# Seven products in four of six feature pairs of the middle tiles, with banks that change parts

## The chip, the cores and the metric

The kernel runs on one core of a Trainium2 chip. A core has five engines that run side by side, each with its own queue of instructions in a fixed order: TensorE (PE; its weight loads are listed as PEld), VectorE (DVE), ScalarE (ACT), GpSimd (POOL) and SyncE (SP, which here only issues DMAs). They meet through semaphores. Matrix products land in PSUM, which has eight banks of 512 fp32 columns on 128 partitions; everything else is in SBUF. The metric is device time in microseconds (us), lower is better. The kernel before took 323.42 us, the median of three runs (322.38, 323.42 and 326.44).

## The reference

Eight batches of eight heads go through sparse attention, and the result through a bilinear feed-forward layer:

```python
scores = scale * np.matmul(q, k.transpose(0, 1, 3, 2))          # (8, 8, 576, 576), head_dim 64
mask_local = (rel >= 0) & (rel < stride)                          # stride 32, heads 0 to 3
mask_strided = (rel >= 0) & (pos[None, :] % stride == pos[:, None] % stride)   # heads 4 to 7
attn = softmax(np.where(masks, scores, -1e9))
x = np.matmul(attn, v).transpose(0, 2, 1, 3).reshape(4608, 512)
a = x @ w_a                                                       # (512, 1536)
b = x @ w_b
out = (a * b) @ w_out                                             # (1536, 512), float32
```

## The kernel before, in words

**Tiles and slots.** The 4608 tokens are nine tiles of 512 (t = 0 to 8). A tile has sixteen slots: twelve for the features f = 0 to 11, 128 features each, in which a and b are made and multiplied into `pf` (`ffn_ab`), and four for the output y (`ffn_ys` for tiles 1 to 8). The attention of batch t + 1 is spread over the slots of tile t. So each engine's queue is one list, written in the order in which the program emits the slots and steps; no planner moves anything.

**Steps of the attention.** `STEPS`, `LATER` and `IN_Y` (lines 578 to 587) give the place of each step. A position is a slot; -4 to -1 are slots of the tile before, and x.5 is the middle of a slot. The letters, with the unit u = 0 to 7 behind them (0 to 3 local heads, 4 to 7 strided ones):
- S: the score products into the banks `st`, three or four of them (line 378), then their exponential on ScalarE (line 398), then the mask, an AND on VectorE of p with the mask (line 416, both in SBUF). "s" is S without the mask, and "m" is the mask alone.
- V: the products with v into bank `o` (line 459); VectorE takes a reciprocal and normalises (lines 467 and 485). For u of 4 and over, `step_VT` writes banks `o` and `e` (line 518), ScalarE takes logarithms and an exponential (530, 531), VectorE multiplies into `xT` (533).
- Q: a copy of query rows from `qT` into `qz` on VectorE (line 334), two for the local heads and two for the strided ones (Q2, Q3).
- O and I: rows out to DRAM and back transposed, both by DMAs of SP.

**a and b.** A plain feature f is four products of 512 columns for a and four for b (line 621), a bank each; in tile 4, whose tokens wrap round in `xT`, each is two products of 256. ScalarE copies a to `a_sb` (line 642), VectorE multiplies it with b (line 645). `mm_bank` (line 607) deals out four banks in turn, three of a pool "mm" and one of a pool "tp"; `o`, `e` and the two of `st` are the other four.

**A seven-product pair.** Features 2g and 2g + 1 form pair g. In `a_pair_mid` (lines 680 to 738) a is made for both features of a pair by seven products of half the contraction and half the tokens (two matmuls of 256 columns each) in place of eight, of sums of weights (`wsum_a`) and differences of x (`xsum`). They go into three half banks: X takes four of the seven in turn, each time copied out by ScalarE into a quarter of `a_sb`; Y takes one, which VectorE adds to quarter (0, 0); Z takes two: the first is copied to `p7`, both are added to quarters of the second feature. b1 and b0 are the b banks of the second and first feature, eight matmuls of 512 columns (line 706). VectorE multiplies `mult(1)` with b1, then `mult(0)` with b0 (line 711). The pair is a generator: its first half, up to `yield p7`, is the slot f = 2g, the rest the slot f = 2g + 1. `MID_A` (line 28) gives pairs 1 and 3 of tiles 3 to 6 this form. Pairs of tiles 7 and 8 have it too, in `a_pair`, a similar function, with no attention beside them and with one addition on GpSimd (line 791).

**y.** It also takes seven products, of stage sums and differences of `pf` that VectorE makes in `fast_s` (line 824; both inputs in SBUF), n = 0 to 3, in slices of the six pairs: [0, 2), [2, 4), [4, 6), some of them as one. Lines 1072 to 1076 and 1122 to 1125 give their slots.

**GpSimd's queue.** GpSimd issues the loads of k, q and v, each behind a copy of one element named `pace` (line 1138), which waits for the slot's last result and so ties the load to the slot. In tiles 3 to 5, slot 2 issues two loads (`kr`, `qr`, line 208), slot 9 one of v (219), slots 11 to 14 four more (237), slot 14 two large ones (210). A pacing copy stands in the queue in each slot that has anything of the tables at the end of the program (`at`, lines 1067 to 1125), stage differences included.

Of the kernel before, what the change touches and what calls it, by code (L numbers as in the profile page):

```python
# [7 lines left out]
F32 = mybir.dt.float32  # L8
BF16 = mybir.dt.bfloat16
I16 = mybir.dt.int16  # L10
ALU = mybir.AluOpType
# [11 lines left out]
PAD = 32  # L23
PW = 344
VW = 128
WCH = (0, 2, 5, 9, 12)
FAST_Y = (1, 2, 3, 4, 5, 6, 7, 8)
MID_A = {t: (1, 3) for t in (3, 4, 5, 6)}
FAST_A = {7: (1, 2, 3, 4, 5), 8: (0, 1, 2, 3, 4, 5)}


# [1 line left out]
def kernel(  # L33
# [10 lines left out]
    nc = tc.nc  # L44
# [6 lines left out]
    KD = d_model // 128  # L51
    FD = d_ff // 128
    TTOK = 512
    NT = n_tok // TTOK
    HL = H // 2
    W = S // 2

    const = ctx.enter_context(tc.tile_pool(name="const", bufs=1))
# [3 lines left out]
    fsb = ctx.enter_context(tc.tile_pool(name="ffn", bufs=2))  # L62
# [3 lines left out]
    psum4 = {}  # L66

    def open_psum(stack, **bufs):
        for nm, n in bufs.items():
# [12 lines left out]
    qT = (const.tile([128, 2, S], BF16, name="qTl"), const.tile([128, HL * W], BF16, name="qTs"))  # L82
    kT_buf = [(const.tile([128, 2, PAD + S], BF16, name=f"kT{i}l"), const.tile([128, 2, RS * GP + 48], BF16, name=f"kT{i}s"))
              for i in range(2)]
    vl_buf = [const.tile([128, HL * 6, VW], BF16, name=f"vl{i}") for i in range(2)]

    p_buf = [const.tile([128, 2, PW], BF16, name=f"p{i}") for i in range(5)]
    vs_buf = [const.tile([NP, HL, RS, VW], BF16, name=f"vs{i}") for i in range(2)]
# [77 lines left out]
    HT = TTOK // 2  # L166
# [5 lines left out]
    def fast_w(n, gs):  # L172
        a, b = ((wov[:, 0, 1], wov[:, 0, 0]), (wov[:, 1, 1], wf[:, 0]), (wov[:, 1, 1], wov[:, 0, 1]),
                (wov[:, 1, 0], wf[:, 1]))[n]
        nc.vector.tensor_tensor(wf[:, n, gs], a[:, gs], b[:, gs], op=ALU.subtract)
# [389 lines left out]
    def F_mm(f, w, kk):  # L565
# [18 lines left out]
    LATER = {-4: "Q0", -3: "Q1", -1: "S0", 0: "S1", 1: "V0", 2: "S2", 3: "V1 Q2 O0", 4: "S3 Q3", 5: "V2", 6: "S4", 7: "V3 O1 I0", 8: "S5", 9: "V4 I1",  # L584
             10: "S6",
             11: "V5"}
    IN_Y = {2: "S7", 6: "V6", 11: "V7"}
    FN = {"Tk": step_Tk, "Tq": step_Tq, "S": step_S, "V": step_V, "X": step_X, "W": lambda b, n: fast_w(n, slice(0, 3)),
          "s": S_px, "m": S_m, "L": lead_vl, "O": rows_out, "I": rows_in, "Pk": lambda b, c: pair_up("k", c), "Pq": lambda b, c: pair_up("q", c),
          "Q": lambda b, n: step_Q(b, n // 2, n % 2)}  # L590
# [6 lines left out]
    steps = {}  # L597

    def take(pos):
        for b, names in steps.get(pos, ()):  # L600
            run(b, names)
# [5 lines left out]
    def mm_bank(shape):  # L607
        nm = "tp" if used[0] % 4 == 3 and used[0] >= 0 else "mm"
        used[0] += 1
        return psum4[nm].tile(shape, F32, tag=nm, name="mm")  # L610
# [13 lines left out]
    def ffn_ab(t, f, mid, ab=None):  # L624
        if f == 0:
            pfs[t] = fsb.tile([128, FD, TTOK], BF16, tag="pf", name="pf", bufs=1)
        pf = pfs[t]
        if f // 2 in FAST_A.get(t, ()) + MID_A.get(t, ()):
            if f % 2 == 0:
                pairs[t, f // 2] = (a_pair_mid if t in MID_A else a_pair)(t, f // 2)  # L630
            return next(pairs[t, f // 2])
        if ab is None:
            ab = [mm_bank([128, TTOK]) for _ in range(2)]
            if f == 0:

                late = 1 if t == 1 else 3
                for kks in ((0, 2, 3), (1,)) if t == 1 else ((0, 2), (1,), (3,)):
                    ab_mm(t, f, ab, kks, last=kks[-1] if kks[-1] == late else -1)
            else:
                ab_mm(t, f, ab, range(KD), mid)  # L640
        a_sb = fsb.tile([128, TTOK], F32, tag="a_sb", name="a_sb", bufs=3)
        nc.scalar.copy(a_sb, ab[0])  # L642
        if t in FAST_Y:
            halves = lambda x: x.rearrange("p (a i s) -> p a i s", i=2, s=16)
            nc.vector.tensor_mul(pf[:, f, :].rearrange("p (i a s) -> p a i s", i=2, s=16), halves(a_sb), halves(ab[1]))  # L645
        else:
            nc.vector.tensor_mul(pf[:, f, :], a_sb, ab[1])
        return pf[:1, f, :1]
# [31 lines left out]
    def a_pair_mid(t, g):  # L680

        pf = pfs[t]
        X = psum4["e"].tile([128, 512], F32, tag="e", name="e")[:, :HT]
        Y, Z, b1, b0 = [mm_bank([128, TTOK]) for _ in range(4)]
        Y, Z = Y[:, :HT], Z[:, :HT]
        a = [fsb.tile([128, TTOK], F32, tag="a_sb", name="a_sb", bufs=3) for _ in range(2)][::-1]
        p7 = fsb.tile([128, HT], F32, tag="p7", name="p7")
        quarter = lambda e, k: a[e][:, HT * k:HT * (k + 1)]

        def P(bank, lhs, rhs, start=False):  # L690
            for c in range(2):
                nc.tensor.matmul(bank, lhsT=lhs(c), rhs=rhs(c), start=start and c == 0, stop=c == 1, skip_group_check=True)  # L692

        w = lambda e, j: (lambda c: wav[:, j, c, g, e])
        ws = lambda n: (lambda c: wsum_a[n][:, c, g])
        x = lambda j, k: (lambda c: x_part(t, j, k)[:, c])
        xs = lambda n: (lambda c: xsum[t][:, n, c])

        def b_mm(bank, e, kks):
            f = 2 * g + e  # L700
            x0 = TTOK * t % (XR * S)
            for kk in kks:
                for k in range(2) if x0 + TTOK > XR * S else (None,):
                    rhs = x_part(t, kk // 2, k)[:, kk % 2] if k is not None else xT[:, kk, x0:x0 + TTOK]
                    dst = bank if k is None else bank[:, HT * k:HT * (k + 1)]
                    nc.tensor.matmul(dst, lhsT=wb_sb[:, kk, 128 * f:128 * (f + 1)], rhs=rhs,  # L706
                                     start=kk == 0 and k in (None, 0), stop=kk == KD - 1 and k in (None, 1))

        def mult(e, bank):
            halves = lambda v_: v_.rearrange("p (a i s) -> p a i s", i=2, s=16)  # L710
            nc.vector.tensor_mul(pf[:, 2 * g + e, :].rearrange("p (i a s) -> p a i s", i=2, s=16), halves(a[e]), halves(bank))

        def add(q, other):
            nc.vector.tensor_tensor(q, other, q, op=ALU.add)

        P(Y, w(0, 1), x(1, 0), True)
        P(X, w(0, 0), x(0, 0), True)
        nc.scalar.copy(quarter(0, 0), X)
        b_mm(b1, 1, (0, 1, 2))
        P(X, ws(1), xs(1))  # L720
        nc.scalar.copy(quarter(1, 0), X)
        P(Z, ws(2), xs(2), True)
        nc.scalar.copy(p7, Z)
        b_mm(b1, 1, (3,))
        add(quarter(0, 0), Y)
        yield p7[:1, :1]
        P(X, ws(0), xs(0))
        nc.scalar.copy(quarter(1, 1), X)
        b_mm(b0, 0, (0,))
        P(Z, w(1, 1), xs(3))  # L730
        add(quarter(1, 0), Z)
        add(quarter(1, 1), p7)
        b_mm(b0, 0, (1, 2, 3))
        P(X, ws(3), x(1, 1))
        nc.scalar.copy(quarter(0, 1), X)
        mult(1, b1)
        mult(0, b0)
        yield pf[:1, 2 * g, :1]

    def a_pair(t, g):  # L740
# [2 lines left out]
        pool, nm = ((pst, "st"), (psum4["o"], "o"))[g % 2]  # L743
        X = pool.tile([128, 512] if nm == "o" else [128, 2, 512], F32, tag=nm, name="ax")
        X = X[:, :HT] if nm == "o" else X[:, 0, :HT]
        a = ([fsb.tile([128, TTOK], F32, tag="a_sb", name="a_sb", bufs=3) for _ in range(2)] if g % 2 == 0 else
             [t.rearrange("p h n -> p (h n)")[:, :2 * TTOK].bitcast(F32) for t in kT_buf[0]])
        got = {k: psum4[nm].tile([128, TTOK], F32, tag=nm, name="mm")
               for k, nm in zip((1, "Z", "Y", 0), (("mm", "mm", "tp", "mm"), ("tp", "mm", "mm", "mm"))[g % 2])}
# [64 lines left out]
    def fast_s(t, n, gs):  # L814
        if t not in pss:
            pss[t] = nat.tile([128, FG * 5 * SW], BF16, tag="shared", name="ps").rearrange("p (n g m) -> p n g m", g=FG, n=5)
        s = pss[t][:, :, gs, :HT]
        x = pfs[t].rearrange("p (g e) (i m) -> p e i g m", e=2, i=2)[:, :, :, gs]
        a, b, op = ((x[:, 0, 1], x[:, 1, 1], ALU.add), (s[:, 0], x[:, 0, 0], ALU.subtract),
                    (x[:, 0, 0], x[:, 0, 1], ALU.subtract), (x[:, 1, 0], s[:, 1], ALU.subtract))[n]  # L820
        if (t, n) == (NT - 1, 2) and {gs.start, gs.start + 1} <= set(FAST_A[t]):
            later[t, gs.start] = lambda: nc.gpsimd.tensor_tensor(s[:, n], a, b, op=op)
            return
        nc.vector.tensor_tensor(s[:, n], a, b, op=op)  # L824
# [156 lines left out]
    with tc.manual_schedule(engines={ENG.PE, ENG.SP, ENG.Pool, ENG.DVE, ENG.Activation}):  # L981
# [76 lines left out]
        for t in range(NT):  # L1058
            slots += [(ffn_ab, t, f) for f in range(FD)] + [(ffn_ys if t in FAST_Y else ffn_y, t, j) for j in range(4)]
        for b in range(1, B):  # L1060
            for pos, names in (STEPS.get(b) or {16 * (b - 1) + x: n for x, n in LATER.items()}).items():
                steps.setdefault(pos, []).append((b, names.split()))
            if b not in STEPS:
                for n, names in IN_Y.items():
                    steps["y", b - 1, n] = [(b, names.split())]

# [53 lines left out]
            for n in range(4):  # L1120
                do(16 * (NT - 1) + 2 * g + 1, fast_s, NT - 1, n, slice(g, g + 1))
        for t in FAST_Y[:-1]:
            for slot, n, z0, z1 in ((4, 0, 0, 2), (5, 2, 0, 2), (6, 1, 0, 2), (7, 3, 0, 2), (8, 2, 2, 4), (9, 0, 2, 4),
                                    (10, 1, 2, 4), (12, 3, 2, 6)):
                do(16 * t + slot, fast_s, t, n, slice(z0, z1))
        for i, (fn, t, j) in enumerate(slots):
# [45 lines left out]
```

## Time and profile before

| | |
|---|---|
| median of three runs | 323.42 us |
| the profiled execution | 322.75 us, span 321.0 us from first to last instruction |
| granted TensorE clock, mean | 0.997 |
| busy: PE, DVE, ACT, POOL | 312.5, 251.3, 193.0, 116.7 us |
| matmuls of line 621, 128 x 512 and 128 x 256 | 480 and 128 |
| matmuls of the eight seven-product pairs, lines 692 and 706 | 112 and 80 |
| VectorE, mean of one: multiplication (645), add of a quarter (714), mask (416), stage difference 512 wide (824) | 681, 414, 452, 418 ns |
| ScalarE, mean of one: copy of 512 (642), of 256 (718), exponential (398) | 585, 372, 650 ns |
| GpSimd, mean of one addition in tiles 7 and 8 (791) | 730 ns |

Rows of a profile name the line of the program, the engine, the operation, and the tile written with the tiles read, as in `mm<-xT,wa_sb`; behind the operation stand the shapes. A timeline row begins with the start and the length in us, and brackets at its end give the idle time of the engine before it and who ended that. In a chain row the first two figures are the start and the time that this piece of the chain holds. The duration of one matmul includes its way through the array, so durations overlap; the step from start to start is what one costs when they follow each other. VectorE and ScalarE also start the next instruction some 0.05 to 0.1 us before the last has ended, where nothing is waited for.

### The profile page before, as it was taken

Reading aid. Unit: us, or ns where it says so; the run is one execution under the profiler, and the core shown is the slowest. Engines: PE = TensorE matmul, PEld = TensorE weight load, DVE = VectorE, ACT = ScalarE, POOL = GpSimd, SP = SyncE. Lnnn points to the kernel's source line nnn. Section 1 sums busy time; section 2 is a strip of 40 time slices with the busy share of each in tenths; the row PEclk is TensorE's granted clock in tenths of the full one; section 3 lists DMA queues with packets and bytes.
Section 4 is the critical chain, followed back from the end, with each engine's and each line's share of the span. In section 5 each row is a group of like instructions: output and inputs, shape, how many; then the busy total and the mean of one; then the engine's idle time right before and its main releaser. Section 6 shows DMA issues by size and latency. Waiting matters only on the chain.

```text
span 321.0 us, 7265 instructions
## 1 busy us (share of the span) xinstructions
PE 312.5 (97%) x2742; PEld 215.5 (67%) x2742; DVE 251.3 (78%) x574; ACT 193.0 (60%) x374; POOL 116.7 (36%) x207
## 2 busy tenths in 40 slices
PE   8799999999999999999999999999999999999994
PEld 5664555455865577567999985569665966786683
DVE  6787886588778898898689868996899668857962
ACT  6873776455754576557655865577556755435541
POOL 8754711780264264315540435033101012203520
PEclk9999999999999999999999999999999999999998
DMA  8999999999399999999999999999153040004004
GB/s 149 176 205 193 204 184 198 203 112 192 61 145 173 261 117 63 126 90 214 142 130 157 191 126 101 102 231 153 12 151 57 2 131 2 0 3 132 0 2 132
DMA packets 127059, 40.31 MB, mean 126 GB/s; under 512 B 114864, under 2 KB 124144, under 8 KB 126832
## 3 DMA queue, kind: packets, MB, share of 16 engines
q0 software_dynamic: 79760, 19.20, 67.7%
q1 hardware_dynamic: 47120, 20.59, 36.4%
q8 instruction: 21, 0.34, 0.5%
q14 instruction: 14, 0.11, 0.1%
q10 hardware_dynamic: 144, 0.07, 0.1%
HBM read 38.93 MB, written 18.28 MB: 178 GB/s over the span
## 4 chain that ended last, share of the span: by engine, by line
PE 92%; DMA 2%; POOL 2%; DVE 1%; ACT 1%; issue 0%; POOLq 0%
PE mm L621 35%; PE mm L890 20%; PE mm L770 6%; PE mm L706 4%; PE st L378 4%; PE mm L952 3%; PE ax L763 3%; PE o L459 2%; DMA tk<-in_v_dram 2%; PE mm L763 2%; PE e L692 2%; PE mm L917 2%; PE mm L692 2%; PE o L518 1%; POOL shared L201 1%; PE end L917 1%
## 5 line engine op out<-in xcount | busy, mean ns | idle before, releaser
L621 PE MATMUL mm<-xT,wa_sb 128*128 128x512 bf16 (+1 forms) x304 | 72.1, 356 | 0.0
L621 PE MATMUL mm<-xT,wb_sb 128*128 128x512 bf16 (+1 forms) x304 | 72.0, 357 | 0.0
L642 ACT COPY a_sb<-mm 128x512 f32<-128x512 f32 x68 | 39.8, 585 | 29.5 <-PE mm L621 26.4
L1138 POOL CAST pace<-pf 1x1 f32<-1x1 bf16 x68 | 19.7, 290 | 88.7 <-DVE pf L645 44.2
L621 PEld LDWEIGHTS <-wb_sb 128*128 128x128 bf16 x304 | 29.3, 98 | 26.5 <-DMA wb_sb<-in_moe_w_b_dram 0.2
L645 DVE TENSOR_TENSOR pf<-a_sb,mm 128x512 bf16<-128x512 f32 x58 | 39.5, 681 | 9.4 <-ACT a_sb L642 5.8
L398 ACT ACTIVATE p<-st 72x576 bf16<-72x576 f32 (+1 forms) x56 | 36.4, 650 | 15.4 <-PE st L378 14.7
L621 PEld LDWEIGHTS <-wa_sb 128*128 128x128 bf16 x304 | 27.3, 98 | 17.4
L890 PEld LDWEIGHTS <-ps 128*128 128x128 bf16 x336 | 32.7, 98 | 3.7
L890 PE MATMUL mm<-wf,ps 128*128 128x256 bf16 x252 | 29.8, 273 | 0.0
L855 ACT COPY y_sb<-mm 128x512 f32<-128x512 f32 (+1 forms) x32 | 17.9, 559 | 19.1 <-PE mm L890 15.7
L1138 POOL COPY pace<-y_sb 1x1 f32<-1x1 f32 x22 | 9.6, 438 | 52.9 <-DVE y_sb L853 27.2
L770 PE MATMUL mm<-xT,wb_sb 128*128 128x512 bf16 x88 | 26.2, 379 | 0.0
L890 PEld LDWEIGHTS <-pf 128*128 128x128 bf16 x252 | 23.5, 98 | 2.7
L237 POOL DMA_DIRECT2D vs<-in_v_dram x24 | 21.7, 907 | 4.6 <-issue 3.1
L890 PE MATMUL mm<-wo_sb,pf 128*128 128x256 bf16 x168 | 21.8, 273 | 0.0
L824 DVE TENSOR_TENSOR ps<-pf 128x512 bf16<-128x512 bf16 (+1 forms) x49 | 19.6, 400 | 0.8
L706 PE MATMUL mm<-xT,wb_sb 128*128 128x512 bf16 (+1 forms) x80 | 19.1, 336 | 0.0
L416 DVE TENSOR_TENSOR p<-p,mask_l 128x576 int16<-128x576 int16 x32 | 14.5, 453 | 5.8 <-ACT p L398 5.5
L533 DVE TENSOR_TENSOR xT<-o,xr 64x288 bf16<-64x288 f32 x16 | 7.7, 480 | 13.5 <-ACT xr L531 13.4
L459 PEld LDWEIGHTS <-p 128*128 128x128 bf16 (+1 forms) x256 | 13.0, 97 | 7.5 <-DVE p L416 1.2
L416 DVE TENSOR_TENSOR p<-p,mask_s 72x576 int16<-72x576 int16 x28 | 12.6, 451 | 1.9 <-ACT p L398 1.7
(211 smaller groups left out, 639.2 us busy)
## 6 DMA issues: line engine op xcount, KB each, us to landing
out_dram<-y_sb SPq DMA_DIRECT2D x14, 512.0 KB, 5.4
kr<-in_k_dram POOLq DMA_DIRECT2D x12, 288.0 KB, 6.9
qr<-in_q_dram POOLq DMA_DIRECT2D x12, 288.0 KB, 8.1
vl<-in_v_dram POOLq DMA_DIRECT2D x6, 384.0 KB, 7.8
out_dram<-y_sb SPq DMA_DIRECT2D x7, 256.0 KB, 3.7
vs<-in_v_dram POOLq DMA_DIRECT2D x24, 72.0 KB, 5.6
xd<-xl SPq DMA_DIRECT2D x12, 144.0 KB, 5.7
wo_sb<-in_moe_w_out_dram POOLq DMA_DIRECT2D x4, 384.0 KB, 11.3
```

The source lines that it names most:

```text
L237: nc.gpsimd.dma_start(out=vs_buf[b % 2][:, h, :, 0:D], in_=v[b, HL + h].rearrange("(p r) d -> p r d", r=RS))
L398: nc.scalar.activation(p_flat(p)[:M, :2 * W].rearrange("p (i n) -> p i n", n=2 * n), st[:M].rearrange("p a (i n) -> p (a i) n", n=256)[:, ...
L416: nc.vector.tensor_tensor(pi, pi, mk, op=ALU.bitwise_and)
L459: nc.tensor.matmul(of[:, j, i, :w], lhsT=pt, rhs=vt, start=True, stop=True)
L621: nc.tensor.matmul(ps_[:, c0:c0 + n], lhsT=w[:, kk, 128 * f:128 * (f + 1)], rhs=xT[:, kk, x0:x0 + n], start=(kk == first and c0 == 0), sto ...
L642: nc.scalar.copy(a_sb, ab[0])
L645: nc.vector.tensor_mul(pf[:, f, :].rearrange("p (i a s) -> p a i s", i=2, s=16), halves(a_sb), halves(ab[1]))
L706: nc.tensor.matmul(dst, lhsT=wb_sb[:, kk, 128 * f:128 * (f + 1)], rhs=rhs, start=kk == 0 and k in (None, 0), stop=kk == KD - 1 and k in (N ...
L770: nc.tensor.matmul(got[e], lhsT=wb_sb[:, kk, 128 * f:128 * (f + 1)], rhs=xT[:, kk, x0:x0 + TTOK], start=kk == 0, stop=kk == KD - 1)
L824: nc.vector.tensor_tensor(s[:, n], a, b, op=op)
L890: nc.tensor.matmul(bank[b][:, q], lhsT=lhs(g, q), rhs=rhs(g), start=k in "172" and q == 0 and g == 0, stop=g == FG - 1, skip_group_check=True)
L1138: nc.gpsimd.tensor_copy(pace, done)
```

## The change

Pairs 1 to 4 of tiles 3 to 6 take the seven-product form, eight pairs more than before. Since such pairs now follow each other, the five banks change parts: Z's bank becomes the next pair's X, X's the next b1, b1's the next Z, while Y and b0 keep theirs; `e` is one of the five. `a_sb` gets a fourth buffer, and the `vl` tiles shrink from 128 to 80 columns. In each of the sixteen pairs the addition of p7 goes from VectorE to GpSimd, and the second Z product moves ahead of b0's first matmul. For the batches beside tiles 3 to 6 the masks of units 2 to 5 move from behind their exponentials into the pairs, between b0 and the last X product; both strided query copies stand behind pair 1 (Q3 stood a slot later); m6 goes from slot 10 to 11. In tiles 1 and 3 to 6 the stage differences of pairs 0 to 3 are taken in one piece, from slot 8 on (in tiles 3 to 6 the first of them inside pair 4, ahead of its multiplications). Pacing copies of slots that have no other entry in the tables fall away.

```diff
-MID_A = {t: (1, 3) for t in (3, 4, 5, 6)}
+MID_A = {t: (1, 2, 3, 4) for t in (3, 4, 5, 6)}
...
-    vl_buf = [const.tile([128, HL * 6, VW], BF16, name=f"vl{i}") for i in range(2)]
+    vl_buf = [const.tile([128, HL * 6, LV], BF16, name=f"vl{i}") for i in range(2)]
...
+    PAIRED = {-4: "Q0", -3: "Q1", -1: "S0", 0: "S1", 1: "V0", 2: "s2", 3: "V1 Q2 Q3 O0", 4: "s3", 5: "V2", 6: "s4", 7: "V3 O1 I0", 8: "s5",
+              9: "V4 I1", 10: "s6", 11: "m6 V5"}
+    IN_P = {1: "m2", 2: "m3", 3: "m4", 4: "m5"}
...
-        X = psum4["e"].tile([128, 512], F32, tag="e", name="e")[:, :HT]
-        Y, Z, b1, b0 = [mm_bank([128, TTOK]) for _ in range(4)]
-        Y, Z = Y[:, :HT], Z[:, :HT]
-        a = [fsb.tile([128, TTOK], F32, tag="a_sb", name="a_sb", bufs=3) for _ in range(2)][::-1]
+        r = [mm_bank([128, TTOK]) for _ in range(4)]
+        r.append(psum4["e"].tile([128, 512], F32, tag="e", name="e"))
+        Y, X, Z, b1, b0 = [r[i] for i in ((0, 2, 4, 1, 3), (0, 4, 1, 2, 3), (0, 1, 2, 4, 3))[(g - 1) % 3]]
+        X, Y, Z = X[:, :HT], Y[:, :HT], Z[:, :HT]
+        a = [fsb.tile([128, TTOK], F32, tag="a_sb", name="a_sb", bufs=4) for _ in range(2)]
...
         P(X, ws(0), xs(0))
         nc.scalar.copy(quarter(1, 1), X)
-        b_mm(b0, 0, (0,))
         P(Z, w(1, 1), xs(3))
         add(quarter(1, 0), Z)
-        add(quarter(1, 1), p7)
-        b_mm(b0, 0, (1, 2, 3))
+        nc.gpsimd.tensor_tensor(quarter(1, 1), quarter(1, 1), p7, op=ALU.add)
+        b_mm(b0, 0, range(KD))
+        take(("p", t, g))
+        if g == 4:
+            fast_s(t, 0, slice(0, 4))
         P(X, ws(3), x(1, 1))
...
-            for pos, names in (STEPS.get(b) or {16 * (b - 1) + x: n for x, n in LATER.items()}).items():
+            for pos, names in (STEPS.get(b) or {16 * (b - 1) + x: n for x, n in (PAIRED if b - 1 in MID_A else LATER).items()}).items():
...
+                for g in MID_A.get(b - 1, ()):
+                    steps["p", b - 1, g] = [(b, IN_P[g].split())]
...
-            for slot, n, z0, z1 in ((4, 0, 0, 2), (5, 2, 0, 2), (6, 1, 0, 2), (7, 3, 0, 2), (8, 2, 2, 4), (9, 0, 2, 4),
+            for slot, n, z0, z1 in (
+                    ((8, 0, 0, 4),) if t == 1 else ()) + ((9, 2, 0, 4), (10, 1, 0, 4), (12, 3, 0, 6)) if t == 1 or t in MID_A else ((4, 0, 0, 2), (5, 2, 0, 2), (6, 1, 0, 2), (7, 3, 0, 2), (8, 2, 2, 4), (9, 0, 2, 4),
                                     (10, 1, 2, 4), (12, 3, 2, 6)):
```

More of the change, by code (lines that the diff above doesn't have):

```diff
@@ L25 @@
 VW = 128
+LV = 80
 WCH = (0, 2, 5, 9, 12)
 FAST_Y = (1, 2, 3, 4, 5, 6, 7, 8)
-MID_A = {t: (1, 3) for t in (3, 4, 5, 6)}
+MID_A = {t: (1, 2, 3, 4) for t in (3, 4, 5, 6)}
 FAST_A = {7: (1, 2, 3, 4, 5), 8: (0, 1, 2, 3, 4, 5)}
@@ L640, in ffn_ab @@
                 ab_mm(t, f, ab, range(KD), mid)
-        a_sb = fsb.tile([128, TTOK], F32, tag="a_sb", name="a_sb", bufs=3)
+        a_sb = fsb.tile([128, TTOK], F32, tag="a_sb", name="a_sb", bufs=4)
         nc.scalar.copy(a_sb, ab[0])
@@ L745, in a_pair @@
         X = X[:, :HT] if nm == "o" else X[:, 0, :HT]
-        a = ([fsb.tile([128, TTOK], F32, tag="a_sb", name="a_sb", bufs=3) for _ in range(2)] if g % 2 == 0 else
+        a = ([fsb.tile([128, TTOK], F32, tag="a_sb", name="a_sb", bufs=4) for _ in range(2)] if g % 2 == 0 else
              [t.rearrange("p h n -> p (h n)")[:, :2 * TTOK].bitcast(F32) for t in kT_buf[0]])
```

## The prediction

> **What bounds the kernel now.** I read the page first (busy shares, slices), then the windows of the tiles that change, then the chain, then the timelines of single engines there.
>
> ```profile
> PE 312.5 (97%) x2742; PEld 215.5 (67%) x2742; DVE 251.3 (78%) x574; ACT 193.0 (60%) x374; POOL 116.7 (36%) x207
> ...
> 127.00:158.30 31.30, 31.30 (x266) 21.54 (x265) 26.63 (x62) 20.40 (x41) 11.84 (x23) 1.00 1.41 142
> 158.30:191.80 33.50, 33.50 (x358) 30.45 (x357) 28.24 (x66) 21.53 (x43) 12.35 (x24) 1.00 1.54 150
> 74.00:78.00 4.00, 3.74 (x26) 1.80 (x25) 3.91 (x11) 2.19 (x4) 0.35 (x2) 1.00 1.31 198
> ```
>
> After a window's length come PE, PEld, DVE, ACT and POOL, then the granted clock. In tiles 3 and 4 TensorE is busy throughout at clock 1.00; its records show no gap from 76 to 288 us. A matmul saved there is time saved, and a wait added there is time lost. A busy PE hides nothing here: start to start, the chain's rows give what one costs.
>
> ```profile
> 140.62 1.73 PE mm L621 x8
> 158.75 1.75 PE mm L621 x16
> ```
>
> 1.73/8 = 0.216 us for 512 columns, 1.75/16 = 0.109 us for 256.
>
> **Products.** A plain pair is 16 x 0.216 = 3.46 us, a seven-product pair 8 x 0.216 + 14 x 0.109 = 3.25 us: 0.20 saved, six times (tiles 3, 5, 6). In tile 4 all are 256 wide: 32 against 30, 0.22 saved, twice. Sum: **-1.65 us**. The instruction order has these counts (36 more matmuls in tiles 3, 5, 6, 4 fewer in tile 4). Weight loads (98 ns) stay under the 109 ns of a matmul; tile 4 already runs so, with PEld 30.45 of 33.5 us.
>
> **Tile 1.** PE's timeline has four 512-column products from 71.45 and from 73.76 us; 0.86 us later the next should start, but V's products start at 72.45 and 75.05: waits of 0.13 and 0.42 us, for masks that stand late in DVE's queue (the 3.74 of 4.00 above). The new order takes four stage differences of about 0.34 us out of the queue ahead of them, three of which stand before the second wait. They come back in slots 8 to 12, where DVE idles 1.2 us (78.7 to 79.9). I take **-0.5 us** of 0 to -0.55.
>
> **What the new pairs wait for.** All four handovers now go from pair to pair. Let S be the end of a pair's score products; 172.14 us in pair 3 of tile 4, the nearest row (ScalarE's timeline there, and GpSimd's in tile 7):
>
> ```profile
> 172.34 0.65 ACT L398 ACTIVATE p<-st 72x576 bf16<-72x576 f32 x1
> 172.88 0.36 ACT L728 COPY a_sb<-e 128x256 f32<-128x256 f32 x1
> ...
> 264.43 0.72 POOL L791 TENSOR_TENSOR kT0s<-kT0s,p 128x256 f32<-128x256 f32 x1 [2.67 <-ACT kT0s L790]
> ```
>
> The exponential ends at S+0.85, the copy that the add to quarter(1,1) needs at S+1.10; GpSimd starts 0.08 later (as in tile 7: copy ends 264.34), S+1.18, and needs 0.72. VectorE's mult(1) starts 0.07 after it (265.22 in tile 7), lasts 0.68, and PE sees it 0.06 later. From S, PE has 1.52 us of the pair left (three products of 0.22, and a b of 0.86), 0.18 of attention (V's six products), and 1.31 until the next pair's Z (three products, three quarters of a b), which takes over mult(1)'s bank: S+3.01. Undisturbed, mult(1) is through at S+2.72. Tiles 7 and 8 run such pairs without a stall, but with no attention beside them. Three things push mult(1) later.
>
> *GpSimd behind VectorE.* GpSimd's one-element copies, which pace the DMAs, show how the two meet:
>
> ```profile
> 175.93 0.17 POOL L1138 CAST pace<-pf 1x1 f32<-1x1 bf16 x1 [3.33 <-DVE rc L467]
> 177.54 0.61 POOL L1138 CAST pace<-pf 1x1 f32<-1x1 bf16 x1 [1.44 <-DVE pf L645]
> ```
>
> ```profile
> 177.33 0.45 DVE L416 TENSOR_TENSOR p<-p,mask_s 72x576 int16<-72x576 int16 x1
> 177.70 0.42 DVE L824 TENSOR_TENSOR ps<-pf 128x512 bf16<-128x512 bf16 x1
> ```
>
> Alone a copy takes 0.17. Started while a mask runs, it takes 0.61 and ends 0.04 after the stage difference that followed the mask back to back; the same 0.61 stands at 106.5, 144.2, 210.9 and 244.2 us. Beside mults and normalisations it stays 0.17. So a GpSimd operation waits for VectorE operations with both inputs in SBUF, and a second one gets in ahead of it. In tile 7 the add that overlaps such a difference by 0.16 takes 0.74, so 0.58 us of it come after the release.
>
> The Trainium skill ("SBUF — State Buffer", Who interferes with whom) says that a VectorE instruction with two SBUF inputs and a GpSimd instruction that reads SBUF contend, and that the first holds the port for its whole length. The copies agree with it. By the rule to the letter all 0.72 of an add would follow the release, 0.14 more in each pair 4: 325.9 in place of the sum below; the 0.74 of tile 7 speaks for 0.58.
>
> In a pair the second add waits for Z (S+0.70), the mask follows 0.33 later and runs S+1.03 to 1.48. The GpSimd add then ends at 2.06 and mult(1) at 2.88: still before 3.01. In **pair 4** the new wide stage difference (the 128x1024 row: 0.68) follows the mask: S+1.40 to 2.08. GpSimd ends at 2.66, mult(1) at 3.42, PE goes on at 3.48. Its bank goes to the b of f = 10, due at S + 1.52 + 0.26 + 0.86 = 2.65. Lost: 0.83 us in each of four tiles, **+3.3**. If the two did not meet, mult(1) would start at 2.0, behind the difference alone, and 0.09 be lost: the ends are 0.4 and 3.3, and I take 3.3, since the copies' rows show the same meeting. mult(0) and ScalarE's copies move along with it; the next to be late would be the b of f = 11, whose bank mult(0) frees 0.66 later, 1.3 us before it is wanted.
>
> *Pair 1 behind the DMA issues.* In tiles 3 to 5 slot 2 issues two loads from GpSimd, and the add now queues behind them:
>
> ```profile
> 165.28 0.51 POOL L208 DMA_DIRECT2D kr<-in_k_dram  x1 [0.30 <-issue]
> 165.77 0.51 POOL L208 DMA_DIRECT2D qr<-in_q_dram  x1
> ```
>
> They end at S+1.78 (S = 164.50). Add 0.58 to 0.72, 0.07, 0.68, 0.06: PE has the bank at 3.17 to 3.31 and wants it at 3.01, +0.16 to +0.30. Nothing else queues there; the pacing copy behind the add waits for mult(0), and pair 2's add comes later than that.
>
> *Two query copies behind pair 1.* From mult(1) at M the queue holds two mults (start to start 0.60 each), reciprocal and normalisation (0.70), two copies (0.84), then pair 2's adds. Y is free at M+3.22, Z's bank (pair 3's X) at M+3.56; with M = S+2.43 that is 5.65 and 5.99, against 5.55 and 5.87 when PE wants them: +0.22. In tile 6, without the loads, about 0.07 in all. For both edits: 3 x 0.45 + 0.07 = **+1.4**, ends 0 and 1.7.
>
> **What costs nothing.** One copy more per pair and its 0.37s (+0.7 us of ScalarE in each of eight pairs) lies in ScalarE's idle third; X's last copy ends 0.62 after the product, the bank is wanted after 0.62, so ScalarE has no reserve there, and any delay passes to PE one to one, twelve times. VectorE gains two adds per new pair, gives the third of each old pair to GpSimd, saves 0.65 per tile by wider differences: within 0.3 us per tile. The masks inside the pairs are wanted a whole pair later. Bank e is read out by the second add at S+1.1, before V4 writes it at S+1.52. Q2's DMA landed in time for the same slot before. No DMA is moved on SP's queue or GpSimd's, except that the 16 adds stand between them: the loads behind have over ten slots until use. The fourth a_sb buffer and the narrower vl tile only make room; vl's rows land in 7.8 us, two tiles ahead.
>
> **Sum**, against the profiled execution (span 321.0, 322.75 with what lies around it; the median of the three is 323.42): -1.65 - 0.5 + 3.3 + 1.4 = +2.55, **325.3 us**, span 323.6. That is 0.8% and inside the 2% that a measurement of this kernel can tell from no change.
>
> **Rivals.**
> - *The meeting in pair 4 doesn't happen* (the add reads before the mask, or the difference slips behind): 322.4. For it: only one-element copies show the double wait. Against: five of five are alike.
> - *No new wait at all:* 322.75 - 2.15 = 320.6, faster. For it: tiles 7 and 8 and the eight old pairs run without a gap. Against: none of these has GpSimd's add beside masks.
> - *The loop through GpSimd is longer than a pair, the slower side.* mult(1) to the next mult(1): 1.21 + 0.70 + 2 x 0.33 + 0.45 + 0.58 + 0.07 = 3.67, and PE's pair is 3.68. From 3.7 on it sets the pace. With whole durations instead of start to start it is 4.07: 0.4 in three loops of four tiles, 4.8 on top, 330. Half of that, 327.7, is likelier.
> - *The clock:* rows: 1.35 us idle within 5 to 10 us, and 0.26 in 74 to 78, at clock 1.00. The lowest that a window shows is 0.78 (after 316 us); at that the sixteen pairs' 59 us would cost 17 more, 342. The Trainium skill ("TensorE: Matmul & The Clock Gate", A second HAM failure mode: psum-queue depth-cycling) has frequent short idles between bank-cycling matmul groups lower the clock, which is this change's pattern; the trace so far speaks against it.
>
> That it does not do what it says, the order of the instructions rules out.
>
> **Chances.** Forecast (324.3 to 326.3) 0.55; pair 4 spared 0.17; no wait 0.13; loop 0.13; clock 0.02. The range 320.5 to 327.5 takes in the first three and part of the loop; without the third it would hold less than 0.8. Over 2% slower (above 329.2): clock and the loop's end, 0.06. Over 2% faster (below 316.3): 0.01, more than every saving named.
>
> **What would show it.** Right: in tiles 3 to 6 GpSimd adds of about 1.4 us in pair 4 and 0.9 elsewhere; PE gaps before the b of f = 10, released by VectorE's mult, 0.8 each, and small ones at pairs 2 and 3 of tiles 3 to 5; no wait at 72 and 75 us. Wrong: adds of 0.74 throughout, a shorter span, gaps at every pair, or a clock below 1.00 before 316 us.

## The result

The changed kernel took **324.18 us**, the median of 21 runs (323.03 to 326.54), beside 322.38 us for the kernel before in as many (321.29 to 327.72): a ratio of **1.0051**, 95% interval 1.0027 to 1.0075. So it is slower, by 1.80 us from median to median, and this is inside the 2% below which two kernels count as the same here. The profiled execution took 325.28 us, span 323.6, against 322.75 and 321.0 before.

The profile after, the page first. GpSimd is busy for 128.6 us in place of 116.7, and each of its 16 additions takes 972 ns on the mean, where one beside no attention took 730. The clock is at 0.9 or more in each of the 40 slices. The rows of the plain a and b now have idle time before them (the last figures, with who ended it), which TensorE could not make up:

```profile
PE 313.5 (97%) x2774; PEld 219.0 (68%) x2774; DVE 252.6 (78%) x562; ACT 196.7 (61%) x398; POOL 128.6 (40%) x202
PEclk9999999999999999999999999999999999999999
L625 PE MATMUL mm<-xT,wa_sb 128*128 128x512 bf16 (+1 forms) x224 | 55.6, 364 | 1.8 <-DMA xT<-xd 1.8
L625 PE MATMUL mm<-xT,wb_sb 128*128 128x512 bf16 (+1 forms) x224 | 55.6, 364 | 1.3 <-DVE pf L716 1.3
L736 POOL TENSOR_TENSOR a_sb<-a_sb,p 128x256 f32<-128x256 f32 x16 | 15.6, 972 | 32.0 <-ACT a_sb L733 22.3
```

(Lines have moved: plain a and b are line 625 now, b of a pair 711, its other products 697, its multiplications 716, its additions 719 on VectorE and 736 on GpSimd, masks 417, stage differences 831.) The two releasers in these rows are the two places to look at. The second is pair 4; its chain in tile 3, from the score products to the b of f = 10:

```profile
143.56 0.26 PE st L379 x4
...
143.84 0.65 ACT p L399
144.49 0.27 ACT a_sb L733
...
144.83 1.51 POOL a_sb L736
...
146.36 0.70 DVE pf L716
...
147.10 1.04 PE mm L625 x4
```

The addition holds 1.51 us of it. VectorE's timeline in the same place says what it waits for; the difference ends at 145.74, and the addition 0.59 us later, at 146.33:

```profile
144.69 0.45 DVE L417 TENSOR_TENSOR p<-p,mask_s 72x576 int16<-72x576 int16 x1
145.06 0.68 DVE L831 TENSOR_TENSOR ps<-pf 128x1024 bf16<-128x1024 bf16 x1
146.36 1.29 DVE L716 TENSOR_TENSOR pf<-a_sb,mm 128x512 bf16<-128x512 f32 x2 [0.62 <-POOL a_sb L736]
```

In tile 5 GpSimd's and VectorE's timelines show the same (an addition of 1.50, the multiplications 0.62 idle before it), but TensorE goes from a to b of f = 10 without a stop, 0.86 us from start to start:

```profile
214.18 1.03 PE L625 MATMUL mm<-xT,wa_sb 128*128 128x512 bf16 x4
215.04 1.03 PE L625 MATMUL mm<-xT,wb_sb 128*128 128x512 bf16 x4
```

Pair 1 of tile 3, in the chain again:

```profile
132.75 0.51 POOL kr L209
133.26 0.49 POOL qr L209
...
133.76 0.76 POOL a_sb L736
...
134.54 0.70 DVE pf L716
...
135.29 0.39 PE mm L697 x2
```

TensorE's waits, as the excess of a step from start to start over 0.216 us for 512 columns or 0.109 for 256 (a step in which the record of a matmul is missing is left out), are in the changed kernel:

| us | Z of pair 2 | pair 3, first products | b of f = 10 | y | sum |
|---|---|---|---|---|---|
| tile 3 | 0.29 | 0.18 + 0.11 | 0.81 | | 1.39 |
| tile 4 | 0.31 | 0.17 + 0.11 | 0.79 | | 1.38 |
| tile 5 | 0.32 | 0.18 + 0.11 | none | | 0.61 |
| tile 6 | none | 0.04 + 0.11 | none | 0.23 | 0.38 |

Now the whole span, by the places where the same score products stand in both traces. They start 0.84 us earlier in the profiled execution of after before anything that was changed (65.74 before, 64.90 after); tile 1 adds -0.33; the start of tile 2 adds +1.98; tile 3 +1.02, tile 4 +0.96, tile 5 +0.22, tile 6 -0.02. Take the waits of the table away from the last four, and -0.37, -0.42, -0.39 and -0.40 remain, -1.58 in all: the products that were saved. What follows the last product, the end of the store, is 0.43 shorter.

The +1.98 is no work of the new pairs. The second half of the transposed x of batch 2 landed late (the chain):

```profile
85.72 7.55 DMA xT<-xd
...
93.32 1.02 PE mm L625 x4
```

Before, the same load took 5.31 us and landed at 91.38, 1.13 us before it was wanted. So that the profiled execution is 2.53 us longer than before's (-0.84, +1.98 and -0.43 among it), and so comes within 0.1 us of the forecast, is luck; the change itself is -0.33 in tile 1 and 3.76 - 1.58 = 2.18 in tiles 3 to 6, **+1.85 us**, which the medians confirm with +1.80.

### The profile page after: what moved, and what is told of

It reads as the page before. It is cut to its first block, busy times and chain, and to the rows that moved or that the text cites. A ratio compares the mean times of both kernels' runs of the same rounds, so it can differ in the third digit from the quotient of the medians.

```text
span 323.6 us, 7321 instructions
## 1 busy us (share of the span) xinstructions
PE 313.5 (97%) x2774; PEld 219.0 (68%) x2774; DVE 252.6 (78%) x562; ACT 196.7 (61%) x398; POOL 128.6 (40%) x202
## 4 chain that ended last, share of the span: by engine, by line
PE 82%; DMA 6%; POOL 4%; DVE 3%; ACT 2%; issue 1%; SPq 0%; POOLq 0%
PE mm L625 25%; PE mm L897 17%; PE mm L777 6%; PE mm L711 5%; PE mm L697 5%; PE st L379 4%; PE mm L959 3%; PE ax L770 3%; PE o L460 2%; DMA xT<-xd 2%; PE mm L770 2%; DMA xd<-xl 2%; DMA vl<-in_v_dram 2%; POOL a_sb L736 2%; PE mm L924 2%; PE end L924 1%
## 5 line engine op out<-in xcount | busy, mean ns | idle before, releaser
L625 PE MATMUL mm<-xT,wa_sb 128*128 128x512 bf16 (+1 forms) x224 | 55.6, 364 | 1.8 <-DMA xT<-xd 1.8
L625 PE MATMUL mm<-xT,wb_sb 128*128 128x512 bf16 (+1 forms) x224 | 55.6, 364 | 1.3 <-DVE pf L716 1.3
L646 ACT COPY a_sb<-mm 128x512 f32<-128x512 f32 x52 | 30.4, 585 | 24.1 <-PE mm L625 21.7
L1148 POOL CAST pace<-pf 1x1 f32<-1x1 bf16 x51 | 16.8, 330 | 53.5 <-DVE pf L649 28.1
L649 DVE TENSOR_TENSOR pf<-a_sb,mm 128x512 bf16<-128x512 f32 x42 | 28.6, 682 | 11.9 <-ACT a_sb L646 8.2
L625 PEld LDWEIGHTS <-wb_sb 128*128 128x128 bf16 x224 | 21.3, 98 | 24.2 <-issue 2.1
L711 PE MATMUL mm<-xT,wb_sb 128*128 128x512 bf16 (+1 forms) x140 | 30.7, 336 | 0.0
L625 PEld LDWEIGHTS <-wa_sb 128*128 128x128 bf16 x224 | 20.2, 98 | 14.3
L1148 POOL COPY pace<-y_sb 1x1 f32<-1x1 f32 x22 | 8.6, 393 | 51.8 <-DVE y_sb L860 27.4
L736 POOL TENSOR_TENSOR a_sb<-a_sb,p 128x256 f32<-128x256 f32 x16 | 15.6, 972 | 32.0 <-ACT a_sb L733 22.3
L716 DVE TENSOR_TENSOR pf<-a_sb,mm 128x512 bf16<-128x512 f32 x28 | 18.1, 682 | 6.3 <-POOL a_sb L736 6.3
L711 PEld LDWEIGHTS <-wb_sb 128*128 128x128 bf16 x160 | 15.6, 98 | 5.7
L831 DVE TENSOR_TENSOR ps<-pf 128x512 bf16<-128x512 bf16 (+2 forms) x39 | 18.1, 463 | 0.7
```

Source lines behind the costliest of these rows:

```text
L625: nc.tensor.matmul(ps_[:, c0:c0 + n], lhsT=w[:, kk, 128 * f:128 * (f + 1)], rhs=xT[:, kk, x0:x0 + n], start=(kk == first and c0 == 0), sto ...
L736: nc.gpsimd.tensor_tensor(quarter(1, 1), quarter(1, 1), p7, op=ALU.add)
L1148: nc.gpsimd.tensor_copy(pace, done)
```

## The experiments

My theory after this: slower by three waits (the addition held up in pair 4, where b1's bank is the next one wanted; pair 1's addition behind two DMA issues; two copies in a row behind pair 1) that outweigh 1.58 us of products. Rivals: that VectorE's queue itself is too long (then moving work in it moves the wait), that tiles 5 and 6 are spared before f = 10 by a lighter attention beside them and not by the bank, and that the late load at tile 2 belongs to the change. The kernels are the changed one with the edits shown; each was timed in five rounds, beside the kernel before. All lie within 2% of it; the interval behind each ratio, some 1 us to either side, says what its time can tell.

**The changed kernel again.**

> The changed kernel once more, unchanged, as the measure for the others. Waits theory (the loss is PE waiting in the pairs of tiles 3 to 6): the same PE gaps as in the first profile, some 1.4 us in tile 3, 1.4 in tile 4, 0.6 in tile 5 and 0.2 to 0.4 in tile 6, ratio to before near 1.005. The wait of 1.98 us for xT's DMA at the start of tile 2 differs from run to run by this theory, anywhere from 0 to 2 us. Boundary theory (the loss is that wait, which comes because PE now reaches tile 2 earlier than the DMA chain): 1.5 to 2.5 us there again.

323.81 us, ratio 1.0060 (1.0020 to 1.0099). The waits are those of the table to 0.02 us, tiles 5 and 6 are without one before f = 10 again, and the additions take 0.75, 0.76, 0.90 and 1.50 in pairs 1 to 4. At the start of tile 2 the wait is 0.21 in place of 1.98: that load took 5.46 us this time. So the waits in tiles 3 to 6 are fixed, and the one at tile 2 is not.

**Pair 4's stage difference behind the multiplications.**

```diff
-        if g == 4:
-            fast_s(t, 0, slice(0, 4))
         P(X, ws(3), x(1, 1))
         nc.scalar.copy(quarter(0, 1), X)
         mult(1, b1)
         mult(0, b0)
+        if g == 4:
+            fast_s(t, 0, slice(0, 4))
```

> The wide stage difference of pair 4 moved from ahead of the two multiplications to behind them. Waits theory: GpSimd's add in pair 4 falls from 1.50 to 0.90 us, the waits of 0.81 and 0.79 us before the b of f = 10 in tiles 3 and 4 go, 1.6 us faster than the changed kernel, some 322.6 us. The waits at pairs 2 and 3 stay. Boundary theory: no change within 0.5 us.

322.35 us, 1.0004 (0.9973 to 1.0036): 1.46 us under the changed kernel in the same series. GpSimd's timeline in pair 4 of tile 3:

```profile
143.33 0.90 POOL L736 TENSOR_TENSOR a_sb<-a_sb,p 128x256 f32<-128x256 f32 x1 [2.79 <-ACT a_sb L733]
```

The addition waits for the mask alone and takes 0.90 in place of 1.50; of the waits of 0.81 and 0.79 before b of f = 10, 0.21 is left in tile 3 and 0.19 in tile 4. In tile 3 that is a step of 1.07 us from a to b in place of 0.86, with all eight matmuls on record (TensorE's timeline):

```profile
143.93 1.03 PE L625 MATMUL mm<-xT,wa_sb 128*128 128x512 bf16 x4
145.00 1.04 PE L625 MATMUL mm<-xT,wb_sb 128*128 128x512 bf16 x4
```

So the difference is worth 0.60 in each of the two places; that the whole 0.8 would go was expected too much. The waits of pairs 2 and 3 stay as they were.

**Something as long in its place, with one input in PSUM.** That the difference delayed the addition by occupying VectorE, and not by its inputs, was still possible. Here a multiplication of the same length stands where the difference stood (a by the bank of b1; nobody reads what it writes), and the difference stands behind.

```diff
+    filler = const.tile([128, TTOK], BF16, name="filler")
...
         if g == 4:
-            fast_s(t, 0, slice(0, 4))
+            nc.vector.tensor_tensor(filler.rearrange("p (k m) -> p k m", k=2), a[0][:, :HT].unsqueeze(1).to_broadcast([128, 2, HT]),
+                                    b1.rearrange("p (k m) -> p k m", k=2), op=ALU.mult)
...
         mult(0, b0)
+        if g == 4:
+            fast_s(t, 0, slice(0, 4))
```

> As the run before, and in the difference's old place an extra multiplication of 0.68 us into a tile that nobody reads, with one input in PSUM and one in SBUF: VectorE's queue ahead of mult(1) is as long as in the changed kernel, but only one input comes from SBUF. Exclusion theory (GpSimd waits out VectorE operations with two SBUF inputs): the add in pair 4 takes 0.90 us and PE waits 0.1 us before the b of f = 10 in tiles 3 and 4, 1.4 us faster than the changed kernel. Queue theory (mult(1) is late since VectorE has 0.68 us more to do ahead of it): the wait stays at 0.8 us whatever the inputs are.

322.53 us, 1.0003 (0.9970 to 1.0036). VectorE's timeline and GpSimd's, pair 4 of tile 3:

```profile
143.85 0.44 DVE L417 TENSOR_TENSOR p<-p,mask_s 72x576 int16<-72x576 int16 x1
144.21 0.68 DVE L741 TENSOR_TENSOR filler<-a_sb,mm 128x512 bf16<-128x512 f32 x1
144.91 1.28 DVE L717 TENSOR_TENSOR pf<-a_sb,mm 128x512 bf16<-128x512 f32 x2
```

```profile
143.98 0.90 POOL L737 TENSOR_TENSOR a_sb<-a_sb,p 128x256 f32<-128x256 f32 x1 [2.79 <-ACT a_sb L734]
```

The addition ends 0.59 after the mask (144.29 to 144.88) although VectorE goes straight on with 0.68 us of other work, and TensorE waits no longer before b of f = 10 than without that work (0.21 in tile 3, 0.20 in tile 4). So it is the two SBUF inputs that hold this addition up. The Trainium skill ("SBUF — State Buffer", Who interferes with whom) states this, and that a VectorE instruction with at most one SBUF input, outside its 2-port modes, does not contend; both halves agree with these rows.

**The additions of p7 on VectorE.**

```diff
-        nc.gpsimd.tensor_tensor(quarter(1, 1), quarter(1, 1), p7, op=ALU.add)
+        add(quarter(1, 1), p7)
```

> One part of the change undone: the addition of p7 in the sixteen pairs back on VectorE, everything else as changed. Waits theory: no add behind the DMA issues or behind a mask; mult(1) of pairs 1 to 3 starts 0.25 to 0.55 us sooner, so the waits at pairs 2 and 3 go (0.58, 0.58, 0.61 and 0.15 us in tiles 3 to 6), and of 0.8 before the b of f = 10 some 0.57 stay in tiles 3 and 4: 2.4 us faster than the changed kernel, some 321.8 us, about 0.2 to 0.6 us faster than before. Rival (VectorE is the nearest bound, 78% busy, and gets 16 adds of 0.33 us more): waits at every pair, not faster than the changed kernel.

321.31 us, 0.9981 (0.9950 to 1.0013): 2.50 us under the changed kernel. All waits behind pair 1 are gone but 0.07 to 0.11 per tile, though VectorE has sixteen additions more. Left are 0.53 and 0.52 before b of f = 10, since the difference still stands ahead of the multiplications (VectorE's timeline, then TensorE's, tile 3):

```profile
142.03 0.43 DVE L719 TENSOR_TENSOR a_sb<-p,a_sb 128x256 f32<-128x256 f32 x1
142.37 0.45 DVE L417 TENSOR_TENSOR p<-p,mask_s 72x576 int16<-72x576 int16 x1
142.74 0.68 DVE L831 TENSOR_TENSOR ps<-pf 128x1024 bf16<-128x1024 bf16 x1
143.34 1.27 DVE L716 TENSOR_TENSOR pf<-a_sb,mm 128x512 bf16<-128x512 f32 x2
```

```profile
144.08 1.04 PE L625 MATMUL mm<-xT,wb_sb 128*128 128x512 bf16 x4 [0.38 <-DVE pf L716]
```

**Both.** The edits of the first and the last together.

> Both edits at once: the addition of p7 is back on VectorE and pair 4's stage difference stands behind the two multiplications. With the additions on VectorE alone, two waits of 0.53 us before b of f = 10 were left; they belong to the difference that still stood ahead of mult(1). My reading: they go, no wait over 0.15 us is left in tiles 3 to 6, and the time is 0.9 to 1.1 us under that of the additions alone, 1.7 to 2.1 us under before (about 0.994). Rival (VectorE has become the bound, so what leaves one place of its queue comes back at the next): not faster than the additions alone, 0.998.

**320.47 us**, 0.9941 (0.9907 to 0.9975): it beats both kernels. VectorE is busy for 258.3 us (81%) in place of 252.6, and no wait above 0.11 us is left in tiles 3 to 6. TensorE at f = 10 of tile 3:

```profile
143.28 1.03 PE L625 MATMUL mm<-xT,wa_sb 128*128 128x512 bf16 x4
144.14 1.03 PE L625 MATMUL mm<-xT,wb_sb 128*128 128x512 bf16 x4
```

The rival of a VectorE that has become the bound falls.

**Both, and Q3 back in slot 4.**

```diff
-    PAIRED = {-4: "Q0", -3: "Q1", -1: "S0", 0: "S1", 1: "V0", 2: "s2", 3: "V1 Q2 Q3 O0", 4: "s3", ...
+    PAIRED = {-4: "Q0", -3: "Q1", -1: "S0", 0: "S1", 1: "V0", 2: "s2", 3: "V1 Q2 O0", 4: "Q3 s3", ...
```

> As the kernel with both edits, and Q3 a slot later, in slot 4 as before the change, so that one query copy in place of two stands behind pair 1's multiplications. If the rest of 0.07 to 0.11 us that was left before Z of pairs 2 and 3 comes from the two copies in a row, it goes: another 0.3 to 0.4 us in the sum of four tiles. If it comes from the additions, nothing changes, and the second copy may make a wait at pair 3 instead.

320.55 us, 0.9937 (0.9906 to 0.9968): the same. The rest is 0.09 to 0.13 us per tile in place of 0.07 to 0.11, so it does not come from two copies in a row.

**The two loads a slot earlier,** the additions on GpSimd and the difference where the change put it.

```diff
-                do(21 if b == FIRST_D + 1 else g0 + 2, load_qk, b, True)
+                do(21 if b == FIRST_D + 1 else g0 + (2 if b == 4 else 1), load_qk, b, True)
```

> The changed kernel with the two loads kr and qr issued one slot earlier (slot 1) in tiles 3 to 5, the additions still on GpSimd. By the prediction's step (pair 1's addition queues behind the two DMA issues) the waits at pairs 2 and 3 of tiles 3 to 5 (0.58 us in each of them, from pair 1's late multiplications and the two query copies) shrink to what tile 6 has, 0.04 and 0.11: pair 1's addition ends 0.3 us sooner after the score products than now. Then 0.4 in each of three tiles, 1.2 to 1.4 us less than the changed kernel, about 1.002 of before. If the two query copies alone make these waits, they stay at 0.29, 0.17 and 0.11, and the time stays at 1.006.

322.67 us, 1.0012 (0.9979 to 1.0044). The waits of tiles 3 to 5 at pairs 2 and 3 fall from 0.58 to 0.61 to 0.11 to 0.16, what tile 6 had from the start, and those before f = 10 stay (0.81, 0.80). GpSimd's timeline in pair 1 of tile 3:

```profile
129.16 0.51 POOL L209 DMA_DIRECT2D kr<-in_k_dram  x1 [0.29 <-issue]
129.65 0.51 POOL L209 DMA_DIRECT2D qr<-in_q_dram  x1
130.15 0.17 POOL L1148 COPY pace<-p 1x1 f32<-1x1 f32 x1
130.64 0.88 POOL L736 TENSOR_TENSOR a_sb<-a_sb,p 128x256 f32<-128x256 f32 x1 [0.32 <-ACT a_sb L733]
```

The addition ends at 131.52, 0.58 after the mask (130.94), and mult(1) can start at 131.56, while TensorE comes to its bank at 132.45; in the changed kernel it started 0.75 us before TensorE went on, and TensorE had to wait. The query copies, still two in a row here, make almost no wait alone; what they add to one that the issues begin, no run separates.

**The loads earlier and the difference behind,** the additions on GpSimd: both edits above.

> Both repairs that leave the additions on GpSimd: pair 4's stage difference behind the multiplications, and the two loads a slot earlier in tiles 3 to 5. Alone they took 1.5 us off the changed kernel each. If the two waits are independent, 2.8 to 3.0 us in sum: left are 0.11 to 0.16 per tile, and the time is about 0.996 to 0.997 of before, 0.5 to 1 us above the kernel with the additions on VectorE and the difference behind. If removing one only uncovers the other, no better than 1.000.

321.16 us, 0.9958 (0.9931 to 0.9985): also faster than before. The two repairs add up.

**Which bank is handed on.** In the changed kernel b of f = 10 takes over b1's bank in tiles 3 and 4, but X's in tiles 5 and 6, where its first matmul waits for ScalarE's copy and not for mult(1): `mm_bank` counts on from tile to tile, so the one bank of the pool "tp" falls on another part of pair 4 in each tile, and the pool "mm" hands out the bank that is released first. One line ahead of pair 1 in each of the four tiles sets the count:

```diff
+        if g == 1:
+            used[0] += (0 - used[0]) % 4
         r = [mm_bank([128, TTOK]) for _ in range(4)]
```

With 0, f = 10 takes X's bank in all four tiles; with 2 in place of 0, b1's.

> The same line with the other remainder: b of f = 10 takes over b1's bank of pair 4 in all four tiles. If the bank decides, waits of about 0.8 us stand before it in tiles 3, 4, 5 and 6: 1.6 us more than the changed kernel, about 1.010 of before; that would be the 3.3 us of the prediction's step for pair 4. Rival: tiles 5 and 6 stay without a wait, 1.005.

b1's bank: 325.44 us, 1.0090 (1.0055 to 1.0125), with waits of 0.80, 0.79, 0.81 and 0.81. The list of waits, and TensorE in tiles 5 and 6:

```profile
PE mm L625 <- DVE pf L718: 2.6, 4, 0.6
```

```profile
213.71 1.04 PE L625 MATMUL mm<-xT,wb_sb 128*128 128x512 bf16 x4 [0.65 <-DVE pf L718]
...
247.56 1.04 PE L625 MATMUL mm<-xT,wb_sb 128*128 128x512 bf16 x4 [0.65 <-DVE pf L718]
```

> The changed kernel with the count of banks set to the same remainder ahead of pair 1 in each of tiles 3 to 6, so that b of f = 10 takes over X's bank of pair 4 in all four of them (in the changed kernel: b1's bank in tiles 3 and 4, X's in tiles 5 and 6). All else stays, the addition of 1.50 us in pair 4 too. If the wait of 0.8 us depends on which bank is handed on, the two of tiles 3 and 4 go and none comes: 1.6 us less than the changed kernel, about 1.001 of before. Rival (in tiles 5 and 6 something else, such as the lighter attention beside them, gives mult(1) its time): the waits of 0.81 and 0.79 stay and the ratio stays at 1.005.

X's bank: 325.33 us, 1.0087 (1.0046 to 1.0128), not less but more. The waits before f = 10 are gone as expected, with the addition still at 1.50; but one of 0.72 to 0.77 us has come at pair 1 in each tile, which neither theory had. The list of waits, then VectorE and TensorE there in tile 3:

```profile
PE mm L713 <- DVE pf L649: 2.4, 4, 0.6
```

```profile
126.92 0.45 DVE L417 TENSOR_TENSOR p<-p,mask_l 128x576 int16<-128x576 int16 x1
127.29 0.42 DVE L680 TENSOR_TENSOR xsum<-xT,xsum 128x512 bf16<-128x512 bf16 x1
...
127.96 0.42 DVE L680 TENSOR_TENSOR xsum<-xT,xsum 128x512 bf16<-128x512 bf16 x1
128.29 0.68 DVE L649 TENSOR_TENSOR pf<-a_sb,mm 128x512 bf16<-128x512 f32 x1
```

```profile
129.03 0.81 PE L713 MATMUL mm<-xT,wb_sb 128*128 128x512 bf16 x3 [0.56 <-DVE pf L649]
```

The same line that moves f = 10 to another bank gives pair 1's b1 the bank that f = 1's multiplication reads, which stands behind a mask and three differences of x. So the bank decides, at both ends of the row of pairs.

**Tile 1 alone,** in the kernel before:

```diff
-            for slot, n, z0, z1 in ((4, 0, 0, 2), (5, 2, 0, 2), (6, 1, 0, 2), (7, 3, 0, 2), (8, 2, 2, 4), (9, 0, 2, 4),
+            for slot, n, z0, z1 in ((8, 0, 0, 4), (9, 2, 0, 4), (10, 1, 0, 4), (12, 3, 0, 6)) if t == 1 else (
+                                    (4, 0, 0, 2), (5, 2, 0, 2), (6, 1, 0, 2), (7, 3, 0, 2), (8, 2, 2, 4), (9, 0, 2, 4),
```

> The kernel before with one part of the change alone: in tile 1 the stage differences of pairs 0 to 3 in one piece, from slot 8 on. The prediction gave this part -0.5 us (of 0 to -0.55); the trace of the changed kernel shows the waits at 72 and 74 us down from 0.13 and 0.42 to 0.13 and 0.09, so 0.33 us less. That is about what five rounds can resolve: expected 0.999 of before, the two waits at 0.13 and 0.09, and no new wait in slots 8 to 12. If the new place costs something there, it shows as a wait between 76 and 84 us and a ratio of 1.000 or more.

322.32 us, 0.9979 (0.9945 to 1.0014): no difference that this can resolve. The waits are 0.13 and 0.09, with none after them up to 84 us, so the expected 0.33 is in the trace but not in the time. Why the first stays can be read from VectorE's timeline:

```profile
71.27 0.69 DVE L645 TENSOR_TENSOR pf<-a_sb,mm 128x512 bf16<-128x512 f32 x1 [0.28 <-ACT a_sb L642]
...
72.56 0.44 DVE L416 TENSOR_TENSOR p<-p,mask_l 128x576 int16<-128x576 int16 x1
```

The mask stands behind a multiplication for which VectorE had to wait 0.28 us, for ScalarE's copy of a. Work that is taken out ahead of that idle time brings the mask no sooner.

**All kernels in one sum.** Each median against the kernel before of its own series, beside -1.58 for the products, -0.33 for tile 1, and that kernel's own waits in tiles 3 to 6 (y's 0.2 among them). The wait at the start of tile 2, different in each profile, is left out:

| kernel | waits in tiles 3 to 6 | sum | measured |
|---|---|---|---|
| changed, first series | 3.76 | +1.85 | +1.80 |
| changed, again | 3.73 | +1.82 | +1.78 |
| difference behind | 2.54 | +0.63 | +0.32 |
| filler | 2.32 | +0.41 | +0.50 |
| additions on VectorE | 1.44 | -0.47 | -0.72 |
| both | 0.40 | -1.51 | -1.88 |
| both, Q3 later | 0.48 | -1.43 | -1.80 |
| loads earlier | 2.40 | +0.49 | +0.32 |
| loads earlier, difference behind | 1.20 | -0.71 | -1.07 |
| b1's bank | 5.12 | +3.21 | +3.21 |
| X's bank | 4.90 | +2.99 | +3.10 |

All eleven lie within 0.4 us of the sum, over a spread of 5.1 us, though each measured difference has an interval of about 1 us to either side; nothing else of size is needed to explain the times.

## Why the prediction came out as it did

The time (324.18 for 325.3) lies in the range of 320.5 to 327.5, though just below the narrower 324.3 to 326.3. The sign is right, and the mechanisms are; three sizes are off, and one event was not foreseen. By its own steps:

- **Products, -1.65:** measured -1.58.
- **Tile 1, -0.5:** the step failed in its size. It took both waits for gone; the first, 0.13, stayed whole, and the second kept 0.09 of 0.42: -0.33. The first is set by ScalarE's copy of a, ahead of which VectorE is idle, and not by the work that was taken out of VectorE's queue.
- **Pair 4, the mechanism:** right. An addition of "about 1.4" is 1.50; 0.58 after the release is 0.59; 0.83 lost is 0.81 and 0.79. By the rule of the Trainium skill ("SBUF — State Buffer", Who interferes with whom) to the letter, the whole 0.72 would follow the release: the measurement decides for less. "0.9 elsewhere" holds in tiles 3 to 5 for pair 3 alone; in pairs 1 and 2 no mask runs beside the addition (0.74 to 0.77). The rival "the meeting in pair 4 doesn't happen" falls, and with it the lower end, 0.4. One inference was too wide, though: that a second VectorE operation with two SBUF inputs gets in ahead of GpSimd. It was read from places with the mask first and the difference second, as in pair 4. Where the difference comes first, at 115.0, 147.9, 181.3, 214.6 and 247.9 us of the trace before, the copy takes 0.36 and ends 0.04 after the difference, so the mask behind it does not hold it up. Why the order matters stays open.
- **Pair 4, the size, +3.3:** this is the term that was mis-sized. "Its bank goes to the b of f = 10, in each of four tiles" holds in two. I followed the handover in one tile and multiplied by four, although `mm_bank` counts on across tiles. Measured: 0.81 + 0.79, and 0.23 in tile 6, where y's first product waits for f = 10's multiplication, late in VectorE's queue: 1.83. With b1's bank in all four it is 3.21, the predicted 3.3.
- **Pair 1 behind the DMA issues and the two copies, +1.4:** measured 1.93 (0.58, 0.59, 0.61 and 0.15). The first part, 0.29 to 0.32, is at the upper end of "0.16 to 0.30": the addition, started at the end of the issues and 0.27 after the mask, takes its whole 0.75, not 0.58. The second, "+0.22", is 0.28 to 0.29. Loads a slot earlier take both away in tiles 3 to 5 but for 0.11 to 0.16.
- **The slower rival, the loop through GpSimd:** falls. It wanted waits at every pair; pair 4's own products show none, and in tile 6 only 0.15 is left.
- **The clock:** 0.9 or more in every slice of the page and 1.00 in the windows of tiles 3 and 4, with four waits of 0.1 to 0.8 in each. The lowering that the Trainium skill ("TensorE: Matmul & The Clock Gate", A second HAM failure mode: psum-queue depth-cycling) describes for frequent short idles between bank-cycling groups is not seen here. The repeat's trace shows 0.59 from 16 to 24 us, long before the new pairs, and 1.00 in tiles 3 and 4; the kernel with tile 1 alone, which has no new pair, shows 0.79 in the same place.
- **"No wait at 72 and 75 us":** half right (0.13 and 0.09).
- **Not foreseen:** the wait of up to 1.98 us for the transposed x at the start of tile 2. In the profiles of the thirteen kernels or repeats here that load takes 4.7 to 7.6 us from issue to landing; it was waited for in eight profiles, all of kernels with tile 1's new order (1.98, 0.84, 0.56, 0.35, 0.21, 0.18, 0.18, 0.09), and not in the kernel before. In four with the new order, tile 1 alone among them, the wait is nothing or 0.02. Over these twelve the mean is 0.37 us, as much as tile 1's gain of 0.33. In all twelve the load is issued only 4.0 to 4.9 us ahead of tile 2's first score products, in the kernel before 5.3; with tile 1 alone, a load as long as before's (5.29 us) keeps 0.09 of the reserve of 1.13. So the new order of tile 1 may cost here what it gains. This is not shown: there is one profile of the kernel before, and the time of tile 1 alone resolves neither.

That the sum (+2.55) came as near to the measured +1.80 as it did owes something to errors of both signs: 1.5 too much for pair 4, against 0.5 too little behind pair 1, 0.2 too much gain in tile 1 and 0.1 in the products.

## What to carry to other kernels

Before work is given to another engine to relieve one, look at what the relieved engine does in the same moment: here VectorE with sixteen additions more is faster by 2.5 us than with GpSimd's help, since GpSimd's additions queue behind its own DMA issues and wait out VectorE's operations on two SBUF inputs. A handover of banks that is worked out in one tile holds in the others only if the count that deals them out repeats with the tile. And where one engine is busy throughout, the sum of its waits from start to start gave the time of these eleven to within 0.4 us, more finely than the interval of any one timing.

## What the runs showed that I had not expected

The exclusion works both ways. In pair 3 of tile 6 of the changed kernel the addition starts before the mask, takes 0.73 as if alone, and it is VectorE's mask that takes 0.80 in place of 0.45 (GpSimd's timeline, then VectorE's):

```profile
242.93 0.73 POOL L736 TENSOR_TENSOR a_sb<-a_sb,p 128x256 f32<-128x256 f32 x1 [3.10 <-ACT a_sb L733]
```

```profile
243.16 0.80 DVE L417 TENSOR_TENSOR p<-p,mask_s 72x576 int16<-72x576 int16 x1
```

It ends 0.30 us after the addition does (243.66 to 243.96), as an addition ends 0.59 after the mask. In the repeat the same place shows the same, 0.72 and 0.80. Whichever comes first keeps its time; in the changed kernel that decides between 0.73 and 1.50 for the same instruction.

One thing the two SBUF inputs do not explain: in the changed kernel a pacing copy that starts beside the attention's multiplications (line 534, one input in PSUM) takes 0.52 in place of 0.17, once in each of tiles 3 to 6, while others beside the same line take 0.18. The runs do not show why.
